# A planned order of instructions, searched again with a smaller margin behind one copy

## The chip, the cores and the metric

One core of a Trainium2 chip runs the kernel. The metric is the device time of one execution in microseconds (us), the median of several runs. A profile is one further execution, recorded by the hardware: its span goes from the first to the last instruction of the program, and its own time is a little longer than its span.

## What is computed

For 2048 tokens of 512 features, float32 throughout, the output mixes two branches by a gate:

```
g = sigmoid((x * gate_w).sum(-1))
a: q = x @ wq in 32 heads of 16; k = x @ wk, v = x @ wv shared by all heads
   p = softmax(q k^T / 4); a = (p v) @ wo
b: h = sigmoid(x @ w_gate) * (x @ w_up)   (1792 wide); b = h @ w_down
out = g * a + (1 - g) * b
```

## The kernel before

**The pieces.** Queries are cut into 4 blocks of 512 tokens and 8 groups of 4 heads, so there are 32 units. For each unit TensorE (PE in the profile) does three things, and a fourth for the feed-forward branch:

- *Maxima* (`maximum`, L1103 to L1110): 64 matmuls of scores, each 128 queries against 512 keys, written to a bank of PSUM; VectorE (DVE) reduces each bank to its row maxima (L1110). When a unit's are done, `max_finish` (L970) joins them, `max_turn` (L975, code T) transposes them on TensorE (L980), and `send_max` puts them under the queries as extra rows, so that the next scores come out with the maximum already subtracted.
- *Scores* (`scores`, L1112 to L1119): 64 matmuls with keys on the partitions; ScalarE (ACT) takes the exp of each bank (L1119) into a tile of SBUF. 21 such tiles exist.
- *Values* (`pv`, L992): for each of 16 chunks of 128 keys, four products of exps and values of 32 columns each (8 matmul records), summed in one bank over the chunks. A chunk is code V in the order.
- *Feed-forward and output projections* (`fill`, L1076 to L1087): float32 products made of three terms, each on one 64-row half of the array.

Maxima, scores and feed-forward use one 64-row half of TensorE each, so two run side by side: a half step. Values use the full height in four column strips. Going from one shape to the other and back takes time, called a round trip below.

**Banks.** PSUM has 8 banks. Each matmul of maxima or scores holds one until VectorE or ScalarE has read it. The two feed-forward halves hold one each for many half steps. A run of value chunks holds one until its sums are written out. `close` (L532) does that: ScalarE copies the bank to SBUF (`sums_out`, L1002; the copy is L1003), and the bank is free. If the unit has an earlier partial sum, GpSimd (POOL) adds the two (`sum_add`, L1005). It happens at the end of a unit's 16 chunks, and earlier wherever the order has the code C.

**The order.** All instructions are issued in one order that is written out in the kernel, `ORDER` (L656), a string of codes. `plan` (L704) steps through it with a `State`, which keeps a clock of its own for each engine, in units of which a half step has 100; `tile_kernel` then issues what it returned. A hexadecimal digit is a half step: its two parts (upper and lower half) are 0 nothing, 1 a maximum, 2 a score, 3 feed-forward. V is a value chunk, G a product of the first stage (keys, queries), T the transpose of maxima, C writes the sums out early, and a dot lets 25 units pass and issues nothing.

**Due times.** The plan's clocks decide which bank a half step gets (`take`, L174: the one that is free first) and when GpSimd's work and the transfers stand in line. The chip's engines still wait for one another by semaphores, so a clock that is wrong changes no result; it changes where the chip waits. The order was found by a search that kept each step from being issued before its bank was free by these clocks. The constants: LATE is the time from TensorE's step to VectorE's or ScalarE's start on the bank, LATE_A the same for an exp; RED, EXP, COPY, SCALED and others the time that an instruction takes up in its engine's queue; TAIL and TAIL_A what follows until it has ended; FREE and FREE_A what follows until TensorE can use the bank again. VALUES is a chunk, IN and OUT are the two changes of shape. `step` (L624) advances the clock; `issue_m`, `issue_s`, `issue_v` and `settle` set when banks come free.

Of the kernel before, what the change touches and what calls it, by code (L numbers as in the profile page):

```python
# [36 lines left out]

LATE, LATE_A, FREE, FREE_A = 190, 200, 65, 60  # L40
# [12 lines left out]

# [600 lines left out]


ORDER = (  # L656
    "GGGGGGGG555G555G555G555GGG5551GG555GG555GG555G555G555G555GT77fff7f7fffff7ffd77ffbf6fedbf7dbfbdbfdf6defedefde7b7b"
# [4 lines left out]
    "bffddd5VVVVC7b677bfefb7e7be7ffddeb7fbbe7ffed6fedfddddVVV996VV6debf7f9fb7bf9db7eff7fbdefe7efedaf7f6fdf5VVC995VVVC"
    "7ebde7fb79fbe7efdedef6b7fb7efd9fbf6edfbff55VVVa9TVVVC76feedbdfe7b7bdbfbd9fb7bf7be7fbdedeedfed7f6V965VVVV6f6fedbd"
    "fbd6fef6bf7bdede7febdbdfbdb7bfef775VVV6a9V999V65aV65aV659VVC7e6bfde7fb7bf6f9bf79fef6f6ffbTbff6ffde6eeddVa69V95aV"
    "95aV955VVVde6eedf7fbdebdbdbfdb7bb7ff6e7ef7e7bdbfff55dVVV96aV9a5VC569VVC9edff6fTffefbfbdb7f5VVC677efef9f6fffdbdbf"
    "faV699VC66ff7bf6f6fb7b7bffde7bfdbbe7ffedef5fdddddVVVVV7a7bfde7fbdedbedfb7ffbf7ef9e7f6faf7f6efddVV95aVVVC7b79fbfb"
    "dafdb7edfedbf6bf79ffe79fef9f6f6feddV9a5VV66TVVVC7b7b7bf9fbdedee7efd6fedbf6ff9f9fb7be7fef5ddVVVVV79bb7fedfb7beded"
    "fb7e7ef6fde7efbd9fedeff7776VVC699VV956VVC7b79fbbdfe7ef9dbbf7ededbbf7ededf6fe7bbffed5VV969VT65VVVC7b7e7bbdfedbb7e"
    "7bfdedeb7bfde7b7fe7ef9efdddeV6a5V65aV95aV56aV952aV999V666V966V996V966V95aV966V995VVC76bff67bfb7bfTffbdbfdedbfeed"
    "fedeedf6fb76fV695VV959VV76bb7ff9fb79fe7bffde7fe7bbdfefedeededff57VV966V996VVVC7bTbffedef9ededfe7fbdffb7bbdfeed7b"  # L670
    "e7ff7b5VVVVCdedebdb7f9fbedf6ff7fbeedff6f6f9f9fbdf7777VVV965VVC6bdff6e7fb7bdee7edfb7b7eff9b7fb7edef6fbddddVVVa95V"
    "VC7b7be7e7fedeedbbdfdbdefbd7bedfefTefbdfb7757VVVVVC7b7ee7edfbdebde7fe7b7b7efdbdbfbdb7edbfefed5VVVVVC7b7bedf9fede"
    "def6fe76fef6fb7f9bf79fbb7ffddd5VV76feb7defbdaf7f9fbd6fdVVVC7adf7ebdfbfTefbdefd776VVVVC7b7eedbdf6fbb7edefdbdfeeff"
    "7bdfbdeb77bff5dVVVVC7b7a7fedfe7edeb7fbd6fb7bff6b7fbdedede7bfdddVVVVV6bdff6b7f9f6feb7dfb6ffb7af7f9fededef9fedf79V"
    "C5a5VVVVC6b5ffeb7fedebdbdbdfbfTbfedef76eff6f9fbdf577VVVVVC7b79bfedfedbf6debf79fe7bf9fedefd6fbdeff7b5bVa96V655VVV"
    "V7b7afdedfe76ffb7bf6f9fe7bdb7e7fbdbfefeddd5eVVV6a9V9T5VVC7b7a7fedf7fbfbe7ffde7fefbf7fdeeffed9fV699V695VVVC7b7bdb"
    "e7fbdef6f6defefb7fb7fedf9fef9dbffdaV969VVVV66ff7bb7f6f6fe7efbdf7eb7ffeedbf7bdffde5ddVVVVC97feedbdfbdebd7bef7efTe"
    "fef9fdbdbf9fbdf77757VVVVVC7e7bed7efb7b7ef9bdfbdedefde7efbdb7bdbfbf6deVV659VV666VVC6dfeb7edfb7afdb7bf79fbbdff6e7d"
    "bfbdef6ffddd9VVa96V966V6a5V955VVVC7b6fb7f9fe7bedf9edfbfTefbdefde7eedeffb7b77aV669V959VV969VVVCdede6fbdf6fee7f6fe"
    "7b7ef9ef7f9efdb7be7ff797bV65aV9a5VV966V996V969V999V666V9a5V969V96aV996VCdedeedf6fedbb7fTfbffdbfbb7defb7e7ef6fb7d"  # L680
    "7VV965VVV7a77bf7efededef9bfdbfbf7f6fbdfe7edbbdf6fdV659VV965VVC66f7fe7efbd9fbbfTfff7bfbe7ef7edee7f9ffd5dVVVVC7b7b"
    "7ef6fedbbddbffdfebb7ff6f9fbd6fedffd5dVVVVVC7b7b7e7bfb7bbdbddefb7eb7e7fdefededef9bfdedeVa95VV659VVVCd6fe7ee7fedeb"
    "dbddbfb7ede7fbdeef7bdbff7b7775VVVVVCd9edfef6fe7e7ebd7bfbfTbfb7efdedef9fef977777VVVVC79eefde7f6febdbdfedbdbf9edfe"
    "7fb7bdbf6ff7775VVV6b7b7fb7fbdef9edfed7ddVVVC7adef7bdfbdebd7bfef7dTVVVC66bffdbdf6fbdebd7bfedfefbdfb7fb7ef67ffddaV"
    "VVVVC7b7b97bffedbb7e7fed9feed7fe7edbfe7bf6fafdddVVVVV7b7b7bf9fbdbf6e7fed6fef6ff9bddefe7bedfedf57VVC595VVVC7b7ee7"
    "efdebdbdef7bdbf9fb77efb79fef6bffed9deVV659VV6T9VVC6edf7ebdfbdee7f6f6fbdbdebfdbdfb7bdbedff777aV655VVVV7b7afd7ef9f"
    "6f7bfe7ef9fe7bf6b7ff9defbfeddd5eVVV6a9V9aTVC566VVC7b7bf7bdfbdefeedefdfffedb7efdfef7f7bbV956VVC796ffef9fb7eb7f9ff"
    "dddaVVC5bfb7e7bfbdeede7f6f7ddVVVV7bdef6b7fb7ef9debdf7f7bfbfedeefd9fedbfd77VVVVC66ffbdbdf6febdbdfe7bedfbd6fbdfb7e"
    "dbedff7677VVVa95VVVC6adff7f6fb7bdeedbdfefTefe7bf7edbf9dbfefb77aV95aV555VVVV76b7fbbdfe7eb7f9ef7e7ededfb7bdef9feb7"
    "ffdddaVC6a5VV956VVVC7bde7eb7fb7bf9bdedfefTbfbdfb767efef6fefede5VV95aV969V666V999VVVC79eff67bfbdeede7fede7ef9b7f7"  # L690
    "bbfd6feedff5b7bV95aV59aVV666V996V969V999V666V9a5V9a5V6a9V996VCde6edff6f9fef6fTfbffdbfb7bbdfbde7e7bfff55VVV695VVd"
    "e7e7bb7f9fbf6f9dbf7fb7fbebfdefdededeff57VV656VV6a5VC7a6ff7f6fedaf7fbTfff7bfbedefd9fedef9ff757VVVCde9eedf7fbdbbdd"
    "bf6f777VVCdbb77bfbd9fef6fededd77VVVVC7b7ba7fdfe7afddedefbdef6fbdf6fb7b7e7bfef6ddVVV99aVVVC9bdff6f9fbdbf6bdefd6fe"
    "de7fef6ef7bfTbfbfd775VVVVC766ffeb7fbdeb7dbbfde7b7eb7fe7dbfe7efbddddddVVVVVC5bfe7eedfe7ebd7b7efedebdb7ff9bf7b7b7e"
    "ffddd5VVV6b7ff9f9fedbf67efbd6feVVC7edafdbdfbdebde7fb7e77VV95TVVVC7b6dfeb7fedbf97bfe7f7bffbedf6fedef9f9ff5dVVVVC7"
    "b7ba7fdfedbb7e7e7f9fe7eff6b7f9fedededbff5dVVVVV7bdef6b7fb7bbdbdefdedbedbf77ef6fbdebdef7df9VVC666VV9T5VVC7b7bf9ed"
    "f6fee7edbfdb7bf9f7ef6f9f6fef9fbfd5dVVVVVC7a5ffbb7fedaf7bdf6f9fbf6f7be7efdedbedf9ff5eV965VVVV76efb7defbdef6b7f9f9"
    "fef9fedb7defbdee7fbf577VVV6a9V696V99TVVC7b7bededf9fffbe7bfdfffe7edefdfbfb7ff6VVC6f6f7bbdfb7bf6e7fdddeeVVVCdb9bf7"
    "bdfb7edee7fe7edbVVVV7b7b6fbdfedbdef9fedffbbdefdf9fe7ef6b7fe7bV69aV9a6Va95V6a6Va6aVV9a6VaaaVVaaTVVbaaVVabffebffaf"
    "bVVfeeffbabbbfbcVVeebbbffffffffeeffbfbfebaVVeeaaVVeaeVeeaVaaaVVaaVeeececcceccc8aaV88888VVVV"  # L700
)


# [517 lines left out]
```

## Time and profile before

| | before |
|---|---|
| median of 3 runs | 1595.2 us (1594.92 to 1595.76) |
| profiled execution, its own time | 1595.86 us |
| its span | 1593.1 us |
| granted TensorE clock | 0.999 |
| records of value matmuls (L995) | 4096, 598 ns each |
| exps (L1119) and reductions (L1110) | 2048 each, 650 and 682 ns |
| copies of sums (L1003), additions (L1006) | 112 and 81 |

How to read it: "line engine op out<-in xcount | busy, mean ns of one | idle before" is a group of instructions of one line of the code. A matmul's record is longer than its place in the array, since matmuls are pipelined and their ends are modelled; starts are what to compare. In a timeline a row gives the start in us from the span's start and the length of a merged group of xcount instructions. Idle time in brackets is that of the row's own engine.

### The profile page before, as it was taken

To read this page: it belongs to the slowest core of one execution; us is meant where nothing else is said; L and a number is where in the kernel's file an instruction comes from. 1 tells how busy PE (TensorE), PEld (TensorE's weight loads), DVE (VectorE), ACT (ScalarE), POOL (GpSimd) and SP (SyncE) were. 2 spreads that over 40 slices of the span, in tenths; PEclk is the share of its full clock that TensorE was granted. 3 is DMA by queue.
4 is the path that set the end of the run, shared out by engine and by line. 5 is a ranking of instruction groups with operands and counts; after the bars stand their busy time and mean duration, and the time that the engine had idled before them with its cause. 6 is when DMAs were issued, how large, how long until landed. Compare 5 with 4: busy or idle time off the path is not lost.

```text
span 1593.1 us, 33707 instructions
## 1 busy us (share of the span) xinstructions
PE 1585.1 (99%) x12950; PEld 1001.1 (63%) x12950; DVE 1393.8 (87%) x2420; ACT 1203.4 (76%) x2356; POOL 877.9 (55%) x680
## 2 busy tenths in 40 slices
PE   9999999999999999999999999999999999999998
PEld 7776666556655666665754666666665466666553
DVE  6899999999899998889899989889998998988842
ACT  5277677788788777778778877778778877677797
POOL 5354554666653476567362648285764357656432
PEclk9999999999999999999999999999999999999999
DMA  7312111142111221124011212114211122111011
GB/s 239 139 51 72 39 60 32 32 121 74 38 59 30 77 72 43 34 64 133 27 55 35 72 40 70 36 45 112 84 41 53 32 76 62 51 32 44 9 37 43
DMA packets 52228, 98.10 MB, mean 62 GB/s; under 512 B 17960, under 2 KB 19240, under 8 KB 51044
## 3 DMA queue, kind: packets, MB, share of 16 engines
q1 hardware_dynamic: 52068, 95.96, 20.4%
q8 instruction: 101, 1.65, 0.5%
q14 instruction: 59, 0.48, 0.1%
HBM read 74.05 MB, written 8.90 MB: 52 GB/s over the span
## 4 chain that ended last, share of the span: by engine, by line
PE 99%; ACT 0%; DVE 0%; issue 0%; DVEq 0%; POOL 0%; ACTq 0%; POOLq 0%
PE bank L1087 31%; PE bank L995 30%; PE bank L1108 17%; PE bank L1117 16%; PE bank L849 4%; PE bank L871 0%; ACT p L1119 0%; PE bank L980 0%; PE bank L1160 0%; PE bank L919 0%; ACT x L767 0%; DVE ba L1169 0%; DVEq L1217 0%; POOL v_aug L865 0%; ACT q L941 0%
## 5 line engine op out<-in xcount | busy, mean ns | idle before, releaser
L1110 DVE TENSOR_REDUCE mx<-bank 128x1 f32<-128x512 f32 x2048 | 1261.3, 682 | 133.9 <-PE bank L1108 62.3
L1119 ACT ACTIVATE p<-bank 128x512 f32<-128x512 f32 x2048 | 1043.8, 650 | 85.7 <-PE bank L1117 46.6
L1117 PE MATMUL bank<-qs,ks 64*128 64x512 f32 x2048 | 710.6, 402 | 0.0
L1108 PE MATMUL bank<-ks,qs 62*128 62x512 f32 x2048 | 688.0, 406 | 0.0
L995 PE MATMUL bank<-p,v_aug 128*32 128x512 f32 x4096 | 487.6, 598 | 0.0
L1108 PEld LDWEIGHTS bank<-ks,qs 62*128 62x128 f32 x2048 | 341.1, 185 | 143.7 <-issue 39.2
L1117 PEld LDWEIGHTS bank<-qs,ks 64*128 64x128 f32 x2048 | 352.0, 185 | 107.1 <-DVE mx L1110 33.7
L1087 PE MATMUL bank<-wd,hl 64*128 64x512 f32 x1344 | 265.2, 393 | 0.0
L995 PEld LDWEIGHTS bank<-p,v_aug 128*32 128x32 f32 x4096 | 109.3, 109 | 244.3 <-issue 218.5
L1003 ACT COPY ou<-bank 128x512 f32<-128x512 f32 x112 | 66.2, 591 | 246.3 <-PE bank L995 185.8
L1087 PEld LDWEIGHTS bank<-wd,hl 64*128 64x128 f32 x1344 | 192.3, 185 | 18.9 <-issue 2.5
L1087 PE MATMUL bank<-xs,wu 64*128 64x512 f32 x672 | 188.7, 394 | 0.0
L1087 PE MATMUL bank<-xs,wg 64*128 64x512 f32 x672 | 183.9, 394 | 0.0
L1087 PE MATMUL bank<-x,wu 64*128 64x512 f32 x672 | 183.0, 391 | 0.0
L1087 PE MATMUL bank<-x,wg 64*128 64x512 f32 x672 | 181.6, 391 | 0.0
L1006 POOL TENSOR_TENSOR ou<-ou,ou 128x512 f32<-128x512 f32 x81 | 104.7, 1293 | 137.1 <-ACT ou L1003 136.7
L967 POOL TENSOR_TENSOR qs<-stage,qs 16x1024 fp32r<-16x1024 f32 x62 | 148.4, 2393 | 4.8
L1071 POOL TENSOR_TENSOR ba<-ba,pa_d 128x512 f32<-128x512 f32 x48 | 61.7, 1288 | 116.7 <-DVE ba L1050 77.6
L1087 PEld LDWEIGHTS bank<-x,wg 64*128 64x128 f32 x672 | 112.5, 185 | 10.5 <-issue 0.8
L1087 PEld LDWEIGHTS bank<-xs,wu 64*128 64x128 f32 x672 | 113.1, 185 | 7.9
L1087 PEld LDWEIGHTS bank<-x,wu 64*128 64x128 f32 x672 | 111.7, 185 | 9.6 <-issue 1.7
L1087 PEld LDWEIGHTS bank<-xs,wg 64*128 64x128 f32 x672 | 110.3, 185 | 7.7
(88 smaller groups left out, 1130.1 us busy)
## 6 DMA issues: line engine op xcount, KB each, us to landing
rg<-wg SPq DMA_DIRECT2D x28, 512.0 KB
ru<-wu SPq DMA_DIRECT2D x28, 512.0 KB
rd<-wd SPq DMA_DIRECT2D x28, 512.0 KB
stage<-qd SPq DMA_DIRECT2D x192, 64.0 KB
xs<-x SPq DMA_DIRECT2D x16, 512.0 KB
xf<-x_in SPq DMA_DIRECT2D x16, 256.0 KB
qd<-q SPq DMA_DIRECT2D x16, 256.0 KB
ra<-wo SPq DMA_DIRECT2D x8, 512.0 KB
```

The source lines that it names most:

```text
L849: nc.tensor.matmul(ps, w[:, p, part(kc)], X[b, kc][:, q, :], start=i == 0, stop=i == 3 * KC - 1)
L967: e.tensor_tensor(qs[r], stage[r], f32(qs[r]), op=ALU.subtract)
L995: nc.tensor.matmul(ps[32 * j:32 * j + 32, :], v_aug[:, c, :], PT.pop((u, c, j)), start=new, stop=last)
L1003: nc.scalar.copy(OU[i], ps)
L1006: nc.gpsimd.tensor_tensor(OU[n], OU[n], OU[i], op=ALU.add)
L1071: nc.gpsimd.tensor_tensor(BA[b, t], BA[b, t], PA.pop((b, t)), op=ALU.add)
L1087: nc.tensor.matmul(banks[i], l, r, start=at == 0, stop=at == j.n - 1)
L1108: nc.tensor.matmul(banks[i], qs_t[u % 3][r, pr, part(qt)], ks[r, kb * 512:(kb + 1) * 512], start=True, stop=True)
L1110: nc.vector.tensor_reduce(MX[u][:, pr, h, qt, kb:kb + 1], banks[i], axis=AX.X, op=ALU.max)
L1117: nc.tensor.matmul(banks[i], ks[r, part(c)], qs_t[u % 3][r, pr, :], start=True, stop=True)
L1119: nc.scalar.activation(p, banks[i], AF.Exp, scale=0.25)
```

## The change

The margin of the copy of the values' sums gets a constant of its own, LATE_V = 60 units instead of LATE = 190; other constants move by a few units; ORDER is replaced as a whole (4961 codes instead of 4907).

```diff
-LATE, LATE_A, FREE, FREE_A = 190, 200, 65, 60
+LATE, LATE_A, FREE, FREE_A = 190, 200, 62, 62
-RED, GATED, SUM, ENDS, PARTS, INVERSE = 260, 258, 285, 60, 325, 70
-EXP, COPY, SCALED = 208, 210, 247
+RED, GATED, SUM, ENDS, PARTS, INVERSE = 258, 258, 285, 60, 325, 70
+EXP, COPY, SCALED = 206, 209, 246
-IN, OUT, VALUES, TURN = 52, 94, 371, 20
+IN, OUT, VALUES, TURN = 52, 94, 370, 20
+LATE_V = 60
...
     def close(self, u, last):
...
-        at = self.on("act", max(self.now + LATE, self.ou_free[i]), COPY) + TAIL_A
+        at = self.on("act", max(self.now + LATE_V, self.ou_free[i]), COPY) + TAIL_A
...
 ORDER = (
-    "GGGGGGGG555G555G555G555GGG5551GG555GG555GG555G555G555G555GT77fff7f7fffff7ffd77ffbf6fedbf7dbfbdbfdf6defedefde7b7b"
-    "defedbf6def9fbdfff575VVVVC7b7bb7edf6fe7bf6f6f9fee7ff9dbdbff7ffdddd5dVVVVVC99ffb7b7fe76fb7ef6f6fe7bfdeedfedbfTefe"
...
+    "GGGGGGGG555G555G555GG555GG555G555GGG555GG555GG555G555G575GTff7ff77fff77fffdf7ffdebdfe7bf7bd7bf9fefdedf9fbf9dbfedd"
+    "bfbdef6f6efdbdfff75VVVC6deedf6fbb7b7fbdb7edbbf77f5dVVC66fe7f9fbdfedfbdf77775VVVC6deefdededee7f6fef9f9bf7bfTfffdf"
...
```

| codes in ORDER | before | after |
|---|---|---|
| half steps (of them with one half empty) | 4258 (16) | 4257 (14) |
| V, in so many runs | 512 in 232 | 512 in 213 |
| changes to the full shape (V or G) | 243 | 224 |
| C | 81 | 100 |
| T | 32 | 32 |
| dots | 0 | 36 |

More of the change, by code (lines that the diff above doesn't have):

```diff
@@ L656 @@
 ORDER = (
-    "GGGGGGGG555G555G555G555GGG5551GG555GG555GG555G555G555G555GT77fff7f7fffff7ffd77ffbf6fedbf7dbfbdbfdf6defedefde7b7b"
-    "defedbf6def9fbdfff575VVVVC7b7bb7edf6fe7bf6f6f9fee7ff9dbdbff7ffdddd5dVVVVVC99ffb7b7fe76fb7ef6f6fe7bfdeedfedbfTefe"
-    "f9f75VVVC7b7b7b7bfedbdbf6ef79fb7bff9b7ffdddd5dVVVV7e7e7ef6fe7efd7bf9fedefdff9effe7eb77bf7fddddddVVVVC7b7b7ee7f9f"
-    "edeb7fbd7ffeefed7bfbdb77fdddddVVVVVC7b7b79fbf6fef6f6fedefTbfedbf76fbf9f6fefdd5dVVVVCd9eeeddffededbf9f6f9feb7fb7b"
-    "db7f6fbdbff775bV595VVV656VVC5eeef7e7fed6fbdefbd9fef6fb7bd7bfbdb7efff57TVVVVC7b7e7eb7f9fbb7f6edfbdbdbdfedeef76fbd"
@@ L662 @@
[L662 to L700, printed above, removed]
+    "GGGGGGGG555G555G555GG555GG555G555GGG555GG555G555G555G575GTff7ff77fff77fffdf7ffdebdfe7bf7bd7bf9fefdedf9fbf9dbfedd"
@@ new lines @@
+    "bfbdef6f6efdbdfff75VVVC6deedf6fbb7b7fbdb7edbbf77f5dVVC66fe7f9fbdfedfbdf77775VVVC6deefdededee7f6fef9f9bf7bfTfffdf"
+    "757dVVVVC6eddeef7b7bf9fbdedef6f9f9feedfdeff777775VVVV67bff5bfbb77bfb79f7dfbfbdbfb7b7d7d7VVVCdeadfdfede7e7eb7fefe"
+    "bdfbd9fddddd.VVVC9e5fefee7deef76ff7b77bVV9T5VVC97b7b7bb7bfdefe7ef6e7e7fedbb7bdf6ffbdedddddd.VVVVVC97ebf7bdbf9edf"
+    "e7eedf6f6fbdebd7bfbdfed6fd7777.VV955VVVC9b7fe7bdb7edef9fbb77bfe7ef9defefTefedefd777VVVVVC67efe79fef6defedb7bf6fe"
+    "db7bf9b7f9ffb7e7fddd5.VVVC6defedb7b7bdbfe7b7fdddVVVV6f9fb7e7bf9dbfe7bdef7f9ffefb7bdedefedbde77VVC9a5VVC6dbb7fb7b"
@@ new lines @@
+    "e7ef7e7edeefdV9T5VV956VVC6f9fede7ebdbdfe7bdbdb7bfedef7bdbedfe7b7e7f57.VVVVVC6db7bf9fbe7e7fe7ef97bf9f9fbbde7fedef"
+    "7ededf75.1VVVVVC6a7ffdeb7b7bfdbdbe7e7f9fbedfeTfef6fef97bfdeVVVVVC97b7bf9fbdef6f6faf7dbf6f6fb7eedf9ffe7bddfdd5.VV"
+    "VVVC7e6f7b7efed9fb7efb7bdaf7edf6fbdb7e7fbfbfe79ff7d5VVV9e67ffbdbdbeV65aV659VVC9debf79fefb9V966V669VC9deedfaffded"
+    "ffb9V65aVTa9V956VVC9b7b7bdfee77ef6f6fefdfbfefd9fbb7f6fedf75ddVVVV6deededeff6f6ff7b7bfdbfbbdfbde7e7efb7bd7f5VVVC9"
+    "5aV995VVC67bfed6fb7efb7edeedfbdefTbfb7fb7bdee7ff7d5dVVVVVC97bfb7b7ebdf9fe7eedededfb7be77bf6ffed9fedf57.VVVVV6ded"
@@ new lines @@
+    "eef7e7bf6fbd9fedbbf7bdbdbdfef6e7f9fb7f67.VVVVVC67e7bf6fb7bf6fededb7bbfd9fbdebdf9ffede7bdfdVV6a5VT5aVV956VVC9deee"
+    "dedfb7dbfbdeb7f9bf7b7bdf6fbbdfe7bdef7d6.V666VC666V699V999V65aVC65aV969V966VC6a6V9aTV999VC966V966VC97bb77efee7b7f"
+    "9fbdff7ebdbfb7b777VVC9e9ffde7eb7defe7bf5f5VVVV6ededffdeedfefedb7fedbb7bdf9fedf5VV596VV966VC97e7bf9fee7b7fb7f77ee"
+    "fbdfbfbfTefefdfd5dddVVVVC99dfbfedb7bedf6feddffefb7bfe7eedbdfb7e7777VVVVVC97bfedbdee77bf6fbedb7bf79fbedfb79ffbfed"
+    "ed5dVVV66dVVC67b7bfb7e7e7efedb7e7bf9fe7eb77fbffdeeddefff75TVVVVVC9edefdededbf9f9fbb77ebfd6fbbd7bf7eeff5ddVVVVC9f"
@@ new lines @@
+    "9fb7e7ee7e7fb7bedb7efdb7bf9f6f9fefdf75ddVVVV67bf6ff7bede7fedbdbedfffebd7fbe7def7bffdd5VVVVVC6daffd6fee77efeb7dbf"
+    "7feffbdbbd7bf6fafdf75VVT9dVVVC67bfe7edbf6f9f6febddbef7bdef9f9f9f7bfe7bfed5.VVa95V665VVV97e9ff6fee7edfb7be7f6fb7b"
+    "7bdbb7fdef6ffdeddd5.VVVCa9TVVVC67bbf7bdbe7e7fe7bbdf9bdf9fee7edfb7fedbfeddd6.VVVVVC6edef7edeb77bfe7ebdf6fb79fb7bf"
+    "f67ebfdbdfddd5.VVVVV679fef6fef9dbfedbf9dbbf7ededeb7f9f7efb7bd7e7.VV696VVC997fefee7f67V6aTVVC9db9ff9fbfe6V95aVC9e"
+    "df6f9ff776VVC97efe79fef5bVVC6b7ef76fe7b7bf9ffdadfffefb76fbf9defe77ddedVVV9dbfbd6fbdebdfe7bbd7bf7f777VVVC9dee7fe7"
@@ new lines @@
+    "e7ffdedd5VVVCTbb7fbfbdadfed7bfedafdedf6ff9ed7bfbf6f6ff57VVVVVC6b7fb7bdbf9edf6feed7bfed9fef9edf9fb7fe7e777d.VVVVV"
+    "67bb7bfde7e7efb7bdbdeb7fe7fbdeededfbd9fffd56.VVVVVC6d6bff6fbdebf7ee7bdfbde7bbdb7fedf9f6fbffed5VVC65aV9aTV956VVVC"
+    "9debfdedbede7fbd6fbdeb7fbdb7bbf7edfb7e7edf76.V666V6a6V999V666V969V996VC699VC95aV96aVT9aV6a5V65aV699VC9b7b7b7fb7e"
+    "f6fe7fd7bfbb7f9fe7bf5VVC6edfe7bdbf6bdf6fbdf5f7VVVV9edededdefeeffededebdfedff7b7775VVV996V65aVC66b7ff6fedbb7fb7ff"
+    "9f7ef9fbfbfTbffddedddddVVVVC667fef6fb7ef9f9f9fbfdffbfe76fef9b7fe7fdd5dVVVVVC97bfe7b7be77efe7af77edef9ffedb6fbd7e"
@@ new lines @@
+    "fbfeedd5.VV955VVVC97bfb7e7bbde7fe7bf9bdedfef9feTfbf6f7ffdedd5VVVVVC69deff6fe7bf9fbdbf67bfb79feedb7f9fedfe7ed7f5."
+    "VVVVVC9edfe7e7e7ebdfbde7e7b7bf6fbb7edfdbf6f9fe7df5.VVV9b7e7fb7be7bfdedbfdddeVVC9e7defbdebdf6fbdefb577VVVVC6fef6f"
+    "bedf6bf79fefTfffebf7b7b7bdefbdffdd5VVVVVC6defbd6fee7b7f9f9febdbfde7bb77bfb7fe7efe5ddd.VVVVV976effedb7ef9f6f6fbf6"
+    "dbfe7bdbfedbdbdfb7ff5d6.VVVVVC67eedfbde7be7f9fef6dbfbdedbbf79fb7fe7e7edbf5..VVa9TVVVVC979fefb7bbdedf6fedb7b7efe7"
+    "bf6defedfbd6fe7d77.VV955VVV97bfb79fee7f9f9fbededfe79fbede7fdbe7fe7b77dd.VVVV669VC6dee7fb7bdbeV9a5VC69ef7feddbbbV"
@@ new lines @@
+    "666V9aTV95aVC67eb7f9ffee9V9a5V966V95aV65aV97ee7fbdbde7V995VVC6deef7e7e7be7fedefddf9febfdbfbf6f9fb77f757VVVVC9b77"
+    "bbb7fdef6f6fefdf9effefd9fef6dbf6fdd777VVVVC9Tefbf7efd9fef9bfdbde7be7f9f6fb7fbf6f6ffdd5VVVVV6eddefbde7ef6fb7bdbe7"
+    "fb7b7b7bfe79fbffed5dddd.VVVVC9a5fffedef6fbdbfTbfe7ef76b7ef7bfbdb7f75dVVVVVC9deff7bdedbf6f9fb7e7e7ef9fef9efd7efb7"
+    "edbdff5f5VVVVVC6b7f9fe7bdeedfbdbf6db7efedbdebdff6ef7b7e7f97.V699V969V65aVC969V65aVC696V969VC699V696V669VT96VVC6b"
+    "7b7fedb7bbdf9ffdfadfeffedbde7bdbf6fedf67VVVVV9debfdb7e7bfb79fbf7f7efefb7edbde7efedeff65VV965VV696VC9e9ff7afdedfb"
@@ new lines @@
+    "7bb7f7ddeVVCTef6fef7e9ff9deff77b57VVVC97b7bfe7bf9dbfe7beddfbffbfde7eede7fb77edddVVVVVC66ff9fe7bf9f6f6fbf6defb79f"
+    "bf6fe7bdfbdafdfe5VVVVVC99ffbf9fbe7f6fe7af7f9ef7e7def9fef9bdffffd5TVVVVC97bb7bb7fdeedfe7edeedbfde7eb7fed9fbdff75f"
+    "77VVVVVC67bfb7b7bdbdbfed6fef9f6f9fee7fbd7ee7fe7f5ddd.VVV9adff7edebd7bfedeb777fVVVC96bdffedee7bdf6ffbf77TVVVC9b76"
+    "ffbdb7ef6fedbf7f7efefbdb7beddbfedff65dVVVVVC69effdbdbdee7fbdbedbdbf7edbedbf7edef7bd77777.VVVVV6a7dffbde7bdefe7bb"
+    "d7edfeb7bf7ef9bdfe7e7efd97.VVVVVC6dbdbfef97bf9fafdf67efbfTbfdefedb7bf6e7f7edVVVVVC6eddeefdbbdb7f9f9fb7bf6fb7b7bb"
@@ L701 @@
+    "7f7efedfdeddd6.VVa65VVVV6b77b7efef67ef9f6fbe7defedbf9bdfb7fbdbfeb7ff5d77VVVC95aVC69deffeb7f9bV996VC6dee7fb7ff65V"
+    "VC9dedeeffbf9fedf6V99TVVC9e76ffbdb7ef6fbd9fe7fbf7effb7f6e7fffdd5ddVVVVV9dedbfede7bbf76fe7bffdfbfbdedbf67bfedefbb"
+    "9VVC6a6V99aV66aVaaaVV9aaVV6a6V6aaVTaVaaaVVbbfefbbbbfVVeafefabfffbfbVVeefeeeffefeffefffffefebfaeVVbbaaVVaabbVVaaa"
+    "8VVaa88...VVeeeeecccecec88888VVVV"
 )
```

## The prediction

> **What bounds the kernel now.** I read the page first: busy time by engine (part 1) and the shares of the chain that ended last (part 4).
>
> ```profile
> span 1593.1 us, 33707 instructions
> ...
> PE 1585.1 (99%) x12950; PEld 1001.1 (63%) x12950; DVE 1393.8 (87%) x2420; ACT 1203.4 (76%) x2356; POOL 877.9 (55%) x680
> ...
> PE 99%; ACT 0%; DVE 0%; issue 0%; DVEq 0%; POOL 0%; ACTq 0%; POOLq 0%
> ...
> L1110 DVE TENSOR_REDUCE mx<-bank 128x1 f32<-128x512 f32 x2048 | 1261.3, 682 | 133.9 <-PE bank L1108 62.3
> L1119 ACT ACTIVATE p<-bank 128x512 f32<-128x512 f32 x2048 | 1043.8, 650 | 85.7 <-PE bank L1117 46.6
> ...
> L1003 ACT COPY ou<-bank 128x512 f32<-128x512 f32 x112 | 66.2, 591 | 246.3 <-PE bank L995 185.8
> ...
> L1006 POOL TENSOR_TENSOR ou<-ou,ou 128x512 f32<-128x512 f32 x81 | 104.7, 1293 | 137.1 <-ACT ou L1003 136.7
> ```
>
> The reader is to see that the chain runs through TensorE for 99% of the span and that no other engine holds a visible share. So the time is TensorE's own work, plus what it loses in changing between its two shapes, plus its waits for banks. The number of matmuls is fixed by the problem. An order can change only the second and the third.
>
> The second view is the timeline of TensorE and its chain, for the price of each piece. Between the end of the first run of value sums and the next run, the old order has 42 half steps (two 64-row matmuls side by side). The first row below is the first of them, the second the value sums that follow. The two rows of the chain are runs of four and of five value chunks.
>
> ```profile
> 97.02 0.50 PE L1108 MATMUL bank<-ks,qs 62*128 62x512 f32 x1
> ...
> 107.02 0.64 PE L995 MATMUL bank<-p,v_aug 128*32 128x512 f32 x4
> ```
>
> ```profile
> 93.52 3.57 PE bank L995 x32
> 107.09 4.43 PE bank L995 x40
> ```
>
> A chunk (8 matmuls) is 4.43 - 3.57 = 0.86 us. The plan counts it as 371 units (370 after), so a unit is 2.32 ns. The 42 half steps take 10.00 us with both changes of shape. Now one round trip on its own: a single chunk between half steps, and the next chunk three half steps later.
>
> ```profile
> 865.77 0.39 PE L1117 MATMUL bank<-qs,ks 64*128 64x512 f32 x1
> 866.09 1.07 PE L995 MATMUL bank<-p,v_aug 128*32 128x512 f32 x8
> 867.09 0.50 PE L1108 MATMUL bank<-ks,qs 62*128 62x512 f32 x1
> ...
> 867.43 0.39 PE L1108 MATMUL bank<-ks,qs 62*128 62x512 f32 x1
> ...
> 867.66 0.39 PE L1108 MATMUL bank<-ks,qs 62*128 62x512 f32 x1
> 867.98 0.64 PE L995 MATMUL bank<-p,v_aug 128*32 128x512 f32 x4
> ```
>
> Past the first, a half step is 0.23 (867.43 to 867.66); the first takes 0.34 and the last 0.32. So the stretch of 42 gives (10.00 - 0.11 - 0.09)/42 = 0.2335 us, 100 units of the plan. From chunk to chunk (866.09 to 867.98) it is 1.89 us. One chunk (0.86) and three half steps (3 x 0.2335 = 0.70) make 1.56. **A round trip between the shapes costs 0.335 us** (1.895 less 1.56). The rows show where: 0.14 behind the chunk, 0.11 in the first half step, 0.09 in the last.
>
> How much is lost in waits? The mean over the 42 half steps is that of one undisturbed half step, so the stretch holds next to none. One kind of wait does show, that of the maxima's transpose for its reduction:
>
> ```profile
> 1007.12 0.40 PE L1108 MATMUL bank<-ks,qs 62*128 62x512 f32 x1
> 1007.63 0.23 PE L980 MATMUL bank<-consts,mm 64*16 64x64 f32 x2
> ```
>
> ```profile
> 1007.26 0.22 DVE L972 TENSOR_REDUCE mm<-mx 128x16 f32<-128x64 f32 x1
> ```
>
> The transpose starts 0.51 us behind the last half step instead of 0.23, and 0.15 behind the reduction's end (1007.48). There are 32 transposes, so such waits are worth 9 us at the very most, and not all are late.
>
> **The change, part by part.** It adds no kind of instruction; it changes numbers in the plan and the order that was searched with them. What the order contains can be counted in its text.
>
> *Round trips.* Runs of half steps between full-shape work: 243 before, 224 after. The value chunks stay 512, in 213 runs instead of 232. 19 round trips at 0.335 are **-6.4 us**, all on the path, since TensorE is the chain.
>
> *Half steps.* 4258 codes before (16 of them with one half empty), 4257 after (14): **-0.2 us**.
>
> *More sums written out early.* The code C stands 100 times instead of 81. Each C is one more copy on ScalarE and one more addition on GpSimd: 19 x 0.59 = 11 us on an engine that is 76% busy and 19 x 1.29 = 25 us on one that is 55% busy. Neither is in the chain, so I count nothing. Without that cover it would be the copy's 0.48 us on ScalarE (below), 9 us.
>
> *Planned waits.* The order has 36 dots of 25 units: 36 x 25 x 2.32 ns = 2.1 us. A dot issues no instruction. It is the plan's clock waiting for a bank, nearly always in front of a run of value chunks. The plan wants the bank free before it counts 52 units (0.12 us) for the change of shape, while the first chunk begins only after that change (0.09 us beyond a half step's 0.23, rows at 867.66 and 867.98). A wait of up to 0.058 us fits inside. Bounds 0 and 2.1, and I take **+0.5**, nearer to the rows that show room.
>
> *The margin of the copy, 190 to 60 units.* This is where cover goes. These rows show two copies; the first half step of the second run precedes its copy, that of the first run is quoted above.
>
> ```profile
> 97.16 0.59 ACT L1003 COPY ou<-bank 128x512 f32<-128x512 f32 x1 [4.35 <-PE bank L995]
> ```
>
> ```profile
> 124.37 0.49 PE L1108 MATMUL bank<-ks,qs 62*128 62x512 f32 x1
> ...
> 124.56 0.59 ACT L1003 COPY ou<-bank 128x512 f32<-128x512 f32 x1 [2.84 <-PE bank L995]
> ```
>
> The first half step follows a chunk's counted end by about 0.12 us (0.14 in the row at 867.09). So the copies start 0.26 and 0.31 after it: 112 and 134 units. The old 190 was 0.13 to 0.18 us too careful; the new 60 (0.14 us) is **0.12 to 0.17 too hopeful**. Two things hang on it.
>
> First the sums' bank. In the plan it was free at 190+210+52+65 = 517 units, and half steps come at 94, 194 and so on, so it could be used by the sixth (594). It is now free at 60+209+52+62 = 383, so from the fourth (394). On the chip the copy ends 0.73 (97.75) to 0.78 us (125.15) behind the first half step, the fourth starts 0.34 + 2 x 0.2335 = 0.80 behind it and the fifth 1.04. How long a release takes, no row shows by itself; the transpose above started 0.15 behind the end it waited for, so 0 to 0.15. At the fifth half step there is no wait; at the fourth 0 to 0.13. Counting banks in the new order's text (two held by the feed-forward halves, five others, then the sums' bank), 32 of the 131 copies (100 C and 31 ends of units) have their sixth bank wanted by the fourth half step or sooner. 32 x 0.02 = **+0.6 us**; bounds 0 and 4.2.
>
> Second ScalarE's queue behind the copy: every exp of the stretch waits there, and the banks of those exps behind it.
>
> ```profile
> 111.58 0.59 ACT L1003 COPY ou<-bank 128x512 f32<-128x512 f32 x1 [3.86 <-PE bank L995]
> 112.06 9.66 ACT L1119 ACTIVATE p<-bank 128x512 f32<-128x512 f32 x19
> ```
>
> The copy holds the queue for 0.48. The new plan has the first exp at 94+200 = 294 units (0.68 us); the chip can start it 0.48 behind the copy's start, at 0.74 to 0.79. The exps run 0.06 to 0.11 us late of the plan. Against this stand 114 units (0.264) that the plan gives from an exp's place in the queue to its bank's reuse. An exp's record lasts 0.650 (row of L1119) and its place 0.477 (next fence), so 0.173 of the 0.264 is used, less the release of 0 to 0.15. I take 0.05 for it: at 0.15 the old order's 112 units would have fallen short everywhere, and TensorE's rows would show it. That leaves 0.04 of reserve, and on average half a half step (0.12) until a bank is wanted. A wait arises where the bank is wanted at once, at most 0.07, and once paid TensorE is back in step. **+1.0 us** over 131 stretches; bounds 0 and 9.
>
> *Clocks near the traced ones.* Spacing of exps (the second row starts 21 exps after the first) and of reductions:
>
> ```profile
> 1567.11 13.84 ACT L1119 ACTIVATE p<-bank 128x512 f32<-128x512 f32 x28
> ```
>
> ```profile
> 1577.12 3.83 ACT L1119 ACTIVATE p<-bank 128x512 f32<-128x512 f32 x7
> ```
>
> ```profile
> 112.02 6.67 DVE L1110 TENSOR_REDUCE mx<-bank 128x1 f32<-128x512 f32 x11 [1.66 <-PE bank L1108]
> ```
>
> An exp's place is (1577.12 - 1567.11)/21 = 0.477 us = 205.5 units: 206 is exact, 208 gave 5 ns of reserve for each exp. A reduction's is (6.67 - 0.68)/10 = 0.599 = 258 units: again the new number is exact. The reserve is gone, but nothing becomes late. I count 0; that it is late is in the range.
>
> At this place a rule of the Trainium skill speaks against the change. "ScalarE: Activation LUTs", section "What ACT_TABLE_LOAD costs", gives an ACTIVATE with immediate scale 186 ns + 0.833 ns an element, and an overlap of about 93 ns back to back: an estimate of 519 ns an exp here, 42 ns more than 206 units. By it the sum would be some 100 us higher, an estimate (131 stretches of 19 exps, 42 ns each); the measured 477 ns contradicts it.
>
> **Sum**: -6.4 - 0.2 + 0.5 + 0.6 + 1.0 = -4.5 us. The profiled execution took 1595.86 us (its span 1593.1 and 2.8 around it), so 1591.4 there; it lay 0.7 above the median of the runs, 1595.2, and against that I forecast **1590.7 us**.
>
> **Rivals.** *Nothing waits at all.* The dots and both margins cost nothing, and fewer transposes come late: 1595.2 - 6.6 = 1588.6, and some 2 us less with the transposes. For it: takes come on a grid of 0.23 us, which hides lags of 0.1. Against: 131 chances to be caught. 0.15.
>
> *The gain is given back.* All dots are paid (2.1), and each of the 131 stretches waits 0.035 us (4.5): 1595.2 - 6.6 + 6.6 = 1595.2. For it: an order searched against too hopeful a clock wants banks just when that clock says so. 0.24.
>
> *Slower: the copy's lag becomes TensorE's wait.* The place is the first take behind each copy that waits for ScalarE's queue. If the full 0.12 to 0.17 us is paid 131 times, that is 18 us: 1595.2 - 6.6 + 2.1 + 18 = 1608.7. It decides from (6.6 + 3.2)/131 = 0.075 us a copy, dots unpaid, or 0.06 with them. For it: the lag is in the rows. Against: the first exp's own lateness hides 0.06 of it. 0.16. By the Trainium skill's spacing in "ScalarE: Activation LUTs" the same mechanism would cost 42 ns for each of 19 exps of the row at 112.06, 0.8 us a stretch; I give that less than 0.01, inside this case.
>
> That the change does nothing is not a case: the runs of chunks are fewer in the text itself.
>
> **How the numbers follow.** About 0.2% (3.2 us) is what a measurement of this kernel can tell from no change. The forecast's own band, 1589.3 to 1592.0, gets 0.45. With the first rival, faster by over 0.2% gets 0.60; within 0.2% 0.24; slower 0.16. The range reaches from the first rival's transposes, 1587.0, to where the slower case begins, 1598.0, leaving out 0.16 above and 0.04 below.
>
> **What would show it.** In the new profile: about 0.86 us a chunk and 0.2335 a half step as before; chunks in 213 runs; copies again 0.14 to 0.19 us behind the first half step; exps in the queue 0.48 behind the copy. If the forecast holds, the first six half steps behind a copy follow each other at 0.23. Wrong would be half steps there of 0.30 or more, a first chunk more than 0.35 behind the last half step where a dot stands, or ScalarE or VectorE with a share in the chain.

## The result: 0.5% slower, with TensorE waiting for ScalarE

| | before | after |
|---|---|---|
| median of 6 runs | 1595.2 us | 1603.1 us |
| ratio, 95% interval | | 1.0050 [1.0037, 1.0063] |
| span of the profiled execution | 1593.1 us | 1601.3 us |

The forecast was 1590.7 us and a gain; measured is a loss of 7.9 us. From `plan` on, line numbers are 2 higher. First the page of after, the lines that answer to those quoted of before:

```profile
span 1601.3 us, 33732 instructions
...
PE 1592.8 (99%) x12950; PEld 1005.5 (63%) x12950; DVE 1393.5 (87%) x2420; ACT 1200.4 (75%) x2375; POOL 901.5 (56%) x699
...
PE 99%; DVE 0%; DMA 0%; ACT 0%; SPq 0%; issue 0%; DVEq 0%; ACTq 0%
...
L1112 DVE TENSOR_REDUCE mx<-bank 128x1 f32<-128x512 f32 x2048 | 1260.8, 681 | 139.5 <-PE bank L1110 72.0
L1121 ACT ACTIVATE p<-bank 128x512 f32<-128x512 f32 x2048 | 1039.9, 675 | 44.3 <-PE bank L1119 25.0
...
L1005 ACT COPY ou<-bank 128x512 f32<-128x512 f32 x131 | 77.4, 591 | 296.4 <-PE bank L997 232.7
...
L1008 POOL TENSOR_TENSOR ou<-ou,ou 128x512 f32<-128x512 f32 x100 | 129.2, 1292 | 192.1 <-ACT ou L1005 191.8
```

The reader is to see how little the page says: TensorE is still 99% of the chain and "busy" 7.7 us longer with the same 12950 matmuls. One number moved much: the idle time in front of ScalarE's exps fell from 85.7 to 44.3 us. More often than before, ScalarE now works on without a pause behind the copy of the sums. (The exps' mean record grew from 650 to 675 ns. Their starts in an unbroken row stay 0.48 us apart, so that an exp's place in the queue is the same.) In the chain, a matmul that starts late is still TensorE's own piece. What it waited for has to be read from the waits of its weight loads (PEld). Before, then after; the columns are us in total, times and the longest:

```profile
PEld bank L1117 <- ACT p L1119: 24.3, 47, 0.8
PEld bank L1108 <- ACT p L1119: 23.7, 40, 0.8
```

```profile
PEld bank L1119 <- ACT p L1121: 43.3, 154, 0.8
PEld bank L1110 <- ACT p L1121: 28.0, 81, 0.8
```

The times are the telling column: the weight loads of maxima and scores were released by an exp 87 times before and 235 times after. (The totals hold the idle time of the loader through a run of value chunks, so they can't be read as loss.) The count says where to look; it is no measure of the loss, as a run below shows. One such wait, in the timelines of TensorE, of its weight loads and of ScalarE:

```profile
191.33 0.39 PE L1089 MATMUL bank<-xs,wg 64*128 64x512 f32 x1
191.43 0.39 PE L1089 MATMUL bank<-x,wg 64*128 64x512 f32 x1
191.56 0.39 PE L1110 MATMUL bank<-ks,qs 62*128 62x512 f32 x1
191.66 0.39 PE L1089 MATMUL bank<-xs,wg 64*128 64x512 f32 x1
...
192.72 0.49 PE L1119 MATMUL bank<-qs,ks 64*128 64x512 f32 x1
192.81 0.41 PE L1089 MATMUL bank<-x,wg 64*128 64x512 f32 x1
193.06 0.39 PE L1089 MATMUL bank<-xs,wg 64*128 64x512 f32 x1
193.06 0.39 PE L1089 MATMUL bank<-x,wg 64*128 64x512 f32 x1
```

```profile
192.72 0.18 PEld L1119 LDWEIGHTS bank<-qs,ks 64*128 64x128 f32 x1 [0.20 <-ACT p L1121]
```

```profile
185.70 0.59 ACT L1005 COPY ou<-bank 128x512 f32<-128x512 f32 x1 [5.19 <-PE bank L997]
186.18 7.47 ACT L1121 ACTIVATE p<-bank 128x512 f32<-128x512 f32 x15
```

```profile
191.44 1.23 ACT L1121 ACTIVATE p<-bank 128x512 f32<-128x512 f32 x2
```

The two exps from 191.44 on end at 192.67; the weight load of the score at 192.72 starts 0.05 us later. The next matmul of that half comes at 193.06, 0.34 behind it instead of 0.2335. The reason is read from the load's row: the wait stands in front of the weight load, which starts together with the matmul's record at 192.72, so the weights aren't there yet when the bank is. **This half of TensorE loses the length of the wait and 0.105 us more**, like the first half step behind value chunks (96.70 to 97.04 in the same trace). ScalarE's rows show that from the copy at 185.70 on it never paused.

Counted in the two traces, matmuls of half steps in mid-stretch whose record lasts 0.47 us or more (such a restart): 15 before and 86 after. Of the 86, an exp had ended 0.04 to 0.09 us earlier in 64, a copy of sums in 9. The loss can also be summed from the starts of the value chunks alone. A stretch between two chunks should take 0.86 us for the chunk, 0.335 for the round trip and 0.2335 for each half step. Against this, the 62 stretches of 25 half steps or more behind a code C (as many in either order) lose 1.1 us in all before and 10.2 after. All stretches together, from the first value chunk to the last, lose 3.2 us before and 16.8 after. These 13.6 us are nearly the whole distance of 14.5 between the new order without any new wait (1588.6) and the measured 1603.1.

### The profile page after: what moved, and what is told of

Same layout as the page of the kernel before. It is cut to its first block, busy times and chain, and to the rows that moved or that the text cites. A ratio compares the mean times of both kernels' runs of the same rounds, so it can differ in the third digit from the quotient of the medians.

```text
span 1601.3 us, 33732 instructions
## 1 busy us (share of the span) xinstructions
PE 1592.8 (99%) x12950; PEld 1005.5 (63%) x12950; DVE 1393.5 (87%) x2420; ACT 1200.4 (75%) x2375; POOL 901.5 (56%) x699
## 4 chain that ended last, share of the span: by engine, by line
PE 99%; DVE 0%; DMA 0%; ACT 0%; SPq 0%; issue 0%; DVEq 0%; ACTq 0%
PE bank L1089 32%; PE bank L997 29%; PE bank L1119 17%; PE bank L1110 17%; PE bank L851 3%; DMA xf<-x_in 0%; DVE mx L1112 0%; PE bank L982 0%; PE bank L1162 0%; ACT x L769 0%; PE bank L921 0%; SPq L754 0%; DVE ba L1171 0%; DVE h L1099 0%; DVEq L1219 0%
## 5 line engine op out<-in xcount | busy, mean ns | idle before, releaser
L1121 ACT ACTIVATE p<-bank 128x512 f32<-128x512 f32 x2048 | 1039.9, 675 | 44.3 <-PE bank L1119 25.0
L1119 PE MATMUL bank<-qs,ks 64*128 64x512 f32 x2048 | 737.5, 409 | 0.0
L1005 ACT COPY ou<-bank 128x512 f32<-128x512 f32 x131 | 77.4, 591 | 296.4 <-PE bank L997 232.7
L1089 PE MATMUL bank<-wd,hl 64*128 64x512 f32 x1344 | 270.5, 392 | 0.0
L1008 POOL TENSOR_TENSOR ou<-ou,ou 128x512 f32<-128x512 f32 x100 | 129.2, 1292 | 192.1 <-ACT ou L1005 191.8
L1089 PE MATMUL bank<-xs,wg 64*128 64x512 f32 x672 | 189.4, 393 | 0.0
```

The lines of the kernel that those rows point to most:

```text
L1005: nc.scalar.copy(OU[i], ps)
L1008: nc.gpsimd.tensor_tensor(OU[n], OU[n], OU[i], op=ALU.add)
L1089: nc.tensor.matmul(banks[i], l, r, start=at == 0, stop=at == j.n - 1)
L1119: nc.tensor.matmul(banks[i], ks[r, part(c)], qs_t[u % 3][r, pr, :], start=True, stop=True)
L1121: nc.scalar.activation(p, banks[i], AF.Exp, scale=0.25)
```

## The experiments

Theory A: the copies start later than the new plan says, ScalarE's queue stays late behind them, and TensorE waits for the exps' banks. Theory B: the reserve that the old, slower clocks for exps and reductions held is gone. Theory C: the sums' own bank is taken too soon. Every run was timed in 5 rounds, with its ratio to the kernel before from runs on the same chip.

**Give ScalarE time back behind the copy.**

```diff
-        nc.scalar.copy(OU[i], ps)
+        nc.scalar.copy(OU[i][:, :256], ps[:, :256])
```

> The changed kernel, but each copy of the values' sums takes only the first 256 of 512 columns (half of the sums is left out), so that ScalarE's queue is free some 0.21 us sooner behind each of the 131 copies; the order is untouched. Theory A (the copy stands in ScalarE's queue 0.12 to 0.17 us later than the plan says, the exps behind it stay late, and TensorE stops for their banks): the half steps of over 0.47 us in mid-stretch fall from 86 to under 30 and the time to 1590 to 1593 us. Theory B (the reserve that the old, slower clocks for exps and reductions gave is gone, wherever they stand): 1600 us or more, the 86 stay. Theory C (only the sums' own bank is taken too soon): the 9 stops right behind a copy go, 1601 to 1602 us.

Measured: 1596.4 us, ratio 1.0009 [1.0000, 1.0017]. 6.7 us of the 7.9 are gone, but it does not reach 1593. Releases of weight loads by exps fall from 235 to 143:

```profile
PEld bank L1121 <- ACT p L1123: 30.8, 88, 0.8
PEld bank L1112 <- ACT p L1123: 22.8, 55, 0.8
```

Restarts fall from 86 to 62, where fewer than 30 were expected. So A holds, and isn't all.

**Make the old order's copies late.**

```diff
+        for _ in range(2):
+            nc.scalar.copy(spent, f32(ks[:, :125]))
         nc.scalar.copy(OU[i], ps)
```

> The kernel before, with two small copies on ScalarE (125 columns each, about 0.3 us of its queue together, nothing reads them) ahead of each of the 112 copies of sums, so that a copy comes about 0.15 us later than the old plan says, as it does in the changed kernel. Theory A: TensorE stops at exps' banks in the long stretches as after the change, 6 to 10 us more, 1601 to 1605 us. Theory B: the old clocks' reserve takes it up, 1595 to 1597 us. Theory C: the sums' bank is wanted 0.48 us behind the copy's end, so no stop there: 1595 to 1597 us.

Measured: 1595.4 us, 1.0000 [0.9991, 1.0009]. This tells nothing of the theories: the experiment did not do what it was for. Its trace shows the two small copies done 3.35 us of idle time ahead of the copy they should have delayed, while ScalarE waited for the value chunks:

```profile
107.53 0.62 ACT L1005 CAST spent<-ks 128x125 bf16<-128x125 f32 x2
111.50 0.59 ACT L1006 COPY ou<-bank 128x512 f32<-128x512 f32 x1 [3.35 <-PE bank L995]
```

It is a control at most: work on ScalarE in the pause ahead of the copy cost nothing here.

**The same two, then one, behind the copy.**

```diff
         nc.scalar.copy(OU[i], ps)
+        for _ in range(2):            # one in the second run
+            nc.scalar.copy(spent, f32(ks[:, :125]))
```

> As the last, but the two small copies stand behind each copy of sums: the sums' bank is free when it was, the exps behind it are 0.3 us later. Theory A: within 1.5 us of the last run, 1600 to 1605 us, since it is the queue and not the sums' bank. Theory C: 1595 to 1596 us, less than the last run. Theory B: 1595 to 1597 us.

> The kernel before with one small copy (125 columns, about 0.27 us of ScalarE's queue, nothing reads it) behind each of the 112 copies of sums, where two (0.53 us) cost 32 us. Theory A with a reserve: two cost 0.29 us a copy, so 0.24 of the 0.53 was covered and one costs about 0.03 x 112 = 3 us, 1597 to 1600 us. If there is no reserve and the price is in proportion: 16 us, 1610 to 1613 us.

Measured: with two 1627.6 us, 1.0204 [1.0190, 1.0218]; with one 1598.1 us, 1.0020 [1.0011, 1.0029]. In the traces the exps behind the copy start 0.53 and 0.19 us later in its queue:

```profile
111.71 0.63 ACT L1006 CAST spent<-ks 128x125 bf16<-128x125 f32 x2
112.24 1.08 ACT L1122 ACTIVATE p<-bank 128x512 f32<-128x512 f32 x2
```

```profile
112.08 0.30 ACT L1005 CAST spent<-ks 128x125 bf16<-128x125 f32 x1
112.27 1.09 ACT L1121 ACTIVATE p<-bank 128x512 f32<-128x512 f32 x2
```

The second small copy waits for the first to end (both write one tile), so one is 0.19 and not the 0.27 that was expected. The first 0.19 us cost 3.0/112 = 0.03 us a copy, the next 0.34 cost 29.5/112 = 0.26. **The old order has a reserve of some 0.2 us behind each copy; past it, about three quarters of each further delay of ScalarE arrives at TensorE.** These are two doses, and nothing between them was measured. Two cost far more than was expected. That the reserve came from the very margins that the change took away is a reading; the new order's own reserve wasn't measured in this way. Releases by exps are 191 and 163 times with two.

```profile
PEld bank L1120 <- ACT p L1122: 54.7, 191, 0.8
PEld bank L1111 <- ACT p L1122: 50.7, 163, 0.8
```

**The new order with an honest margin in the choice of banks** (LATE_V = 120, and where no bank is free by the plan, the one that is free first).

> The changed kernel's order with the margin of the copy at 120 units, as traced, instead of 60; where the order then wants a bank that the plan does not have free, it takes the one that is free first. Only the choice of banks can change, the order of the instructions that TensorE, ScalarE and VectorE run through does not. Theory A: the exps behind the copy are as late as before, so 1600 to 1603 us. Theory B: no change, 1602 to 1604 us. Theory C: the sums' bank is no longer taken too soon, 1594 to 1597 us.

Measured: 1602.6 us, 1.0048 [1.0034, 1.0061]. C falls: it's the order of the work, not which bank is taken. A and B both allow this time. The run also shows what the count of releases is worth:

```profile
PEld bank L1117 <- ACT p L1119: 30.7, 85, 0.8
PEld bank L1108 <- ACT p L1119: 27.4, 76, 0.8
```

Exps release 161 weight loads instead of 235, while the time is nearly that of the changed kernel. By a count a little wider than the one above, its restarts even rise from 91 to 118. So the number of waits alone does not give the loss.

**Reductions 5 columns shorter, then tiny copies, then both.**

```diff
-        nc.vector.tensor_reduce(MX[u][...], banks[i], axis=AX.X, op=ALU.max)
+        nc.vector.tensor_reduce(MX[u][...], banks[i][:, :507], axis=AX.X, op=ALU.max)
...
-        nc.scalar.copy(OU[i], ps)
+        nc.scalar.copy(OU[i][:, :64], ps[:, :64])
```

> The changed kernel with each reduction over 507 of 512 columns (five keys of each bank are left out of the maxima), which gives VectorE about 5 ns per reduction, what the old clock of 260 units gave over 258. Theory A (ScalarE's lateness behind the copies): 4 of 86 stops were VectorE's alone, so under 1 us less, 1602 to 1603.5 us. Theory B (the reserve of the old clocks is missing): 2 to 5 us less, 1598 to 1601 us.

> The changed kernel with copies of the sums of 64 of 512 columns (seven eighths of the sums are left out), which gives ScalarE's queue some 0.37 us back behind each copy, where 256 columns gave 0.21 and took 6.7 us off. Theory A: stops for exps, 35 left at 256 columns, fall under 15; 1590 to 1594 us. Theory B: what is left at 256 columns has to do with VectorE's and the exps' own clocks: 1595 to 1597 us.

> The changed kernel with copies of 64 columns and reductions over 507 (both parts left out as in the two runs above). Theory A: as with the tiny copy alone within 1 us. Theory B: 2 us or more under it. Either way it shows how near the order comes to 1588.6 us, the sum without any new wait.

Measured: 1603.5 us, 1.0053 [1.0039, 1.0066], with shorter reductions; 1596.5, 1.0009 [1.0000, 1.0018], with tiny copies; 1595.1, 1.0002 [0.9993, 1.0010], with both. VectorE's lost reserve is worth nothing while ScalarE is late and 1.3 us when it isn't. A copy of 64 columns gives no more than one of 256, against the expected 1590 to 1594 us: the copies' lateness is worth 6.6 us and is used up, and something else holds the order at 1596.

**Readers out of the way, in a fixed rotation of tiles.** Exps and reductions over 432 of 512 columns, alone and together, in the new order, and together in the old one. For exps that write only a part, the 21 tiles were kept and used in turn.

> The changed kernel with exps over 432 of 512 columns (the last 80 are left at ones; the 21 exp tiles are kept in fixed rotation for that), some 0.067 us less of ScalarE's queue per exp; copies are whole. Theory A2 (all that is left after the copies' 6.6 us, too, are TensorE's waits for ScalarE, since a score's exp starts 0.54 us behind it where the plan's 200 units say 0.46): 1589 to 1593 us. Theory D (what is left are VectorE's and TensorE's own): 1595 to 1597 us.

> The changed kernel with reductions over 432 of 512 columns (80 keys of each bank are left out of the maxima), some 0.083 us less of VectorE's queue each. Theory A: VectorE stops TensorE seldom, 1599 to 1602 us, as five columns gave nothing by themselves and 1.3 us with tiny copies. Theory D: 1595 to 1597 us.

> The changed order with both readers out of the way (exps and reductions over 432 columns, parts left out as in the two runs above). What is left is TensorE's own time: 1586 to 1590 us. If waits for DMAs or GpSimd or the planned dots hold it up: 1592 us or more.

> The old order with the same parts left out of exps and reductions. If a round trip between TensorE's shapes costs 0.335 us, it is 6.6 us (19 trips and one half step) above the run with the new order and both readers short, give or take 1: 1592.5 to 1596 us. If the trips are worth nothing: within 1 us of that run.

Measured: 1593.7 us, 0.9993 [0.9984, 1.0001], with short exps; 1602.0, 1.0050 [1.0037, 1.0062], with short reductions; 1590.0, 0.9966 [0.9952, 0.9979], with both; and the old order with both 1599.0, 1.0026 [1.0016, 1.0036], slower than with whole readers. The rotation did that: a tile came up before its value chunk had been read, and chunks then waited inside their runs, by the starts in the trace 7.4 us in the old order and 3.2 in the new. Only the run with short reductions, which needs no rotation, can be used. Its ratio is that of the changed kernel, 1.0050, so VectorE by itself holds nothing that can be told from zero.

**The same, with each exp in the tile that was read longest ago**, and exps over 506 columns by themselves, which gives back what the old clock of 208 units gave over 206.

```diff
-        p = PT[u, c, 2 * pr + h] = ap.tile([P, 512], F32, tag="p", ...)
-        nc.scalar.activation(p, banks[i], AF.Exp, scale=0.25)
+        p = PT[u, c, 2 * pr + h] = LEFT.pop(0)      # pv puts it back once read
+        nc.scalar.activation(p[:, :506], banks[i][:, :506], AF.Exp, scale=0.25)
```

> The old order with exps and reductions over 432 of 512 columns (the rest left out), now with each exp in the tile that a value chunk read longest ago, so that no chunk waits inside its run as with the fixed rotation, where 12 such waits made up 7.4 us. Without them 1599.0 becomes 1591.6: 1590 to 1593 us.

> The new order with the same left out and the same choice of tiles: 1590.0 less 3.2 us of such waits, 1586 to 1588 us. If a round trip is worth 0.335 us, 6.6 us under the old order with both readers short, give or take 1.5; if the trips are worth nothing, the same as it.

> The new order with exps alone over 432 columns (the rest left out), whole reductions and whole copies. Theory A2 (all lost time is TensorE waiting for ScalarE): 1588 to 1591 us. Theory D (the rest beyond the copies' 6.6 us is VectorE's or TensorE's own): 1594 to 1597 us.

> The new order with exps over 506 columns (six left out), 5 ns each, what the old clock of 208 units gave over 206. Theory B for the exps: the reserve grows with each exp, about 0.05 us by the eleventh, where most stops are, so 3 to 6 us less, 1597 to 1600 us. If the lost clock reserve does not matter: 1602 to 1603.5 us.

Measured: old order, both short, 1590.6 us, 0.9971 [0.9959, 0.9982]; new order, both short, 1586.3, 0.9944 [0.9931, 0.9956]; new order, exps short, 1590.6, 0.9971 [0.9961, 0.9981]; new order, exps over 506, 1598.1, 1.0018 [1.0009, 1.0027]. With exps out of the way, releases of weight loads by exps fall from 235 to 40:

```profile
PEld bank L1111 <- ACT pp L1129: 17.0, 21, 0.8
PEld bank L1120 <- ACT pp L1129: 15.3, 19, 0.8
```

So ScalarE carries 1603.1 - 1590.6 = 12.5 us of the new order's time. Not all of it is new: with both readers short the old order gains 4.6 us as well, and the new one 16.8, so the readers cost the new order 12.2 us more than the old. Six columns of each exp, 5 ns, are worth 5.0 us: B holds for ScalarE. The other choice of tiles can't be what did it: the steps from chunk to chunk inside a run, 299 in the new order, add up to 259.8 us in the traces of the changed kernel, of short exps and of exps over 506 alike. And with its readers out of the way the new order is faster: 4.25 us under the old.

**Both of ScalarE's causes at once, and a copy that VectorE shares.** The second run leaves nothing out.

```diff
-        nc.scalar.copy(OU[i], ps)
+        nc.scalar.copy(OU[i][:, :256], ps[:, :256])
+        nc.vector.tensor_copy(OU[i][:, 256:], ps[:, 256:])
```

> The new order with copies of 256 columns and exps over 506 (the rest of both left out). If the copies' lateness (6.7 us) and the exps' lost reserve (5.0 us) are two losses: 1603.1 - 11.7, 1590.5 to 1592.5 us, which is also what exps out of the way gave. If both only ease the same lateness: 1593.5 to 1596 us.

> The new order with each copy of sums split: 256 columns on ScalarE, the other 256 on VectorE. Nothing is left out. ScalarE's queue gets the 0.21 us back that took 6.7 us off. If VectorE's part (some 0.33 us of its queue each) lies in its idle time behind a run of value chunks: 1596 to 1598 us. If VectorE, 87% busy, is late in turn: its stops for reductions rise and the time is 1602 us or more.

Measured: copies of 256 and exps of 506 columns 1593.0 us, 0.9984 [0.9976, 0.9993]: 10.1 us of the 11.7 that the two give one by one, between the two expectations. They are two causes with a small part in common, and together they come near the 12.2 us by which the readers cost the new order more. The split copy is 1626.6 us, 1.0199 [1.0185, 1.0213]: VectorE has no room behind the value chunks, and the stops move to its reductions (and, fewer, to its part of the copy):

```profile
PEld bank L1120 <- DVE mx L1113: 59.8, 151, 0.8
PEld bank L1111 <- DVE mx L1113: 51.3, 126, 0.8
```

No kernel that computes everything was faster than the one before.

## Why the prediction was wrong, point by point

- **Round trips, -6.4 us.** Right. The short stretches show the price without much else in it: those of up to nine half steps (122 before, 86 after, without a transpose) take 0.008 and 0.006 us less each than 0.335 and 0.2335 a half step say. With both readers short the new order is 4.25 us faster by the medians and 5.3 by the two profiled executions (1590.43 and 1585.1), where 6.6 were reckoned with the half step. Of what is missing, 1.0 us are waits that the new order's trace holds more of, from the first chunk to the last; the rest is open.
- **C codes, nothing.** The 19 additions on GpSimd show up nowhere in the chain. ScalarE's 19 further copies weren't tried by themselves, so what part of the copies' 6.6 us is their number and what part their lateness stays open (the plan does count each copy's time in the queue).
- **Dots, +0.5.** Within the bounds, at their lower end. By the starts in the trace, the 32 runs of chunks right behind dots start 0.326 us behind the last matmul of the half steps in the mean, and the 180 other runs 0.319 behind: 0.2 us in all.
- **The copies' start.** Right: 0.14 us behind the first half step at the first copy after (below), and 0.18 in the median of all 131, so that most copies lie at the upper end of the 0.12 to 0.17 us that were called too hopeful.

```profile
96.70 0.50 PE L1110 MATMUL bank<-ks,qs 62*128 62x512 f32 x1
```

```profile
96.84 0.58 ACT L1005 COPY ou<-bank 128x512 f32<-128x512 f32 x1 [3.31 <-PE bank L997]
```

- **The sums' bank, +0.6.** Right in size: 9 restarts came right behind a copy; the choice of banks gave 0.5 us (1602.6 against 1603.1).
- **ScalarE's queue behind the copy, +1.0: this is the step that failed.** The runs say 6.6 us, inside the bounds of 0 to 9 but far from the value taken. Two things in its working were off. It took a wait to cost what is missing; a wait like the one shown above costs its half 0.105 us more, since the weights weren't loaded ahead of it. And it let half a half step hide the lag on average. A reading, not tested by itself, is that a search that ends when every bank is free just at the time the clock says leaves no lag for an average to hide.
- **Clocks near the traced ones, 0.** The numbers were right (exps 0.477 us), the conclusion wrong: "the reserve is gone, but nothing becomes late". 5 ns an exp were worth 5.0 us, because the restarts came mostly in mid-stretch (24 of them with the eleventh exp behind the copy), where 5 ns an exp have grown to 0.05. With exps of 506 columns those 24 fall to 8. They are the second half of the miss.
- **The rivals.** The slower one named the right mechanism; the threshold was 0.06 to 0.075 us a copy. Measured is (7.9 + 6.6)/131 = 0.11, below the full 0.12 to 0.17, and 5.0 us of it are the exps' clock. Without that part, with exps over 506 columns, the order still takes 1598.1 us, just where this rival was to begin. Its place was wrong: it put the waits at the first take behind the copy that waits for ScalarE, and only 4 restarts came with the first exp. Its chance of 0.16 was too small: the row that showed the copies late was in hand, and the reserve against it was put together from averages. The rule of the Trainium skill's "ScalarE: Activation LUTs", section "What ACT_TABLE_LOAD costs", by which an exp takes an estimated 519 ns, has no part in it: the spacing after is again 0.478 us ((191.44 - 186.18)/11, the starts of the first and the twelfth exp in the rows above).
- **What would show it.** Of the signs that were named as wrong, the first came true in kind, half steps of 0.30 or more behind waits, but only about a fifth of them lie in the first six half steps, where they were looked for; the others come further on. The second, a first chunk more than 0.35 behind the last half step where a dot stands, came once in 32 (0.44). The last did not come true: ScalarE got no share in the chain, because a late weight load is booked on TensorE.

What is left open: copies of 256 and exps of 506 columns together leave 1593.0 us, 4.4 above the forecast without any new wait (1588.6). VectorE's reductions are likely part of it: with ScalarE's exps out of the way they hold 4.2 us (1590.6 against 1586.3). How much of that the old order had too wasn't measured. That 1586.3 lies under 1588.6 is no contradiction, since 1588.6 still holds the 4.6 us that the readers cost the old order.

## What to carry to other kernels

In an order that is planned against clocks, a margin that looks too long may be the only reserve of what stands behind it; change one clock at a time, and ask what a queue has left at the end of its longest unbroken row, not on average. To find out, delay the suspect in small doses: the reserve is where the cost turns from nothing to nearly one to one. Where an engine is 99% busy before and after, don't look for the loss in the shares of busy time. Who released its weight loads, and how often, says where to look; how much was lost is summed from the starts, or read from a run that takes the suspect away.

## What the runs showed of the hardware

- A wait in front of a half-array matmul cost that half 0.105 us beyond its length: the next matmul of that half followed at 0.34 us and not 0.2335, with the weight load starting with the release (192.72 and 193.06 above).
- An exp's end released a weight load within 0.05 us (192.67 to 192.72).
- The two halves of TensorE run apart: their matmuls start 0.10 and 0.13 us from each other in turn ahead of the stop (191.33 to 191.66 above) and together behind it (both at 193.06). That one half's short wait is hidden by such a lead is a reading, not measured by itself.
- Small copies of 125 columns on ScalarE have a record of 0.30 us. Of two that write one tile the second starts 0.33 us behind the first (0.63 less 0.30, the row at 111.71), while one by itself takes 0.19 of the queue (112.08 to 112.27).
